# Dilated and sliding attention into a swish layer: the first batch's dilated values used where they land, one load for the tail values, and a new set of scheduling biases

## The chip, the cores and the metric

The kernel runs on one core of a Trainium2 chip. The metric is the device time of one execution in microseconds (us). The core has a matrix engine (TensorE, PE in the profile, with its weight loads as PEld), a vector engine (VectorE, DVE), a scalar engine (ScalarE, ACT), a general engine (GpSimd, POOL) and an engine that here only issues transfers (SyncE, SP). TensorE writes into eight banks of PSUM; the other tiles lie in SBUF. Transfers that change the type from float32 to bfloat16 are issued by POOL, the others by SP.

## What is computed

There are 8 batches of 8 heads, 576 positions and 64 numbers per head. Four heads look at the last 32 positions, four at every fourth one of the last 128. The result is the input of a layer 512 -> 2048 -> 512 with a swish that has its own beta for each of the 2048.

```python
scores = scale * np.matmul(q, k.transpose(0, 1, 3, 2))
rel = pos[:, None] - pos[None, :]
mask_plain = (rel >= 0) & (rel < window)                                   # heads 0 to 3, window = 32
mask_dil = (rel >= 0) & (rel < window * dilation) & (rel % dilation == 0)  # heads 4 to 7, dilation = 4
scores = np.where(masks[None, :, :, :], scores, -1000000000.0)
attn = np.exp(scores - max) / (sum + 1e-09)
x = np.matmul(attn, v)            # then to (4608 tokens, 512)
h = x @ w_in
g = h * (1.0 / (1.0 + np.exp(-beta * h)))
out = g @ w_out
```

## The kernel before

**Two kinds of work share TensorE.** The layer is cut into nine token tiles of 512. For each tile, 16 slots of four matmuls (L901, 512 columns) make h; ScalarE takes a tanh of each slot (L910) and VectorE multiplies (L915) into `g_t`, of which there are two. Then 4 blocks of 16 matmuls (L936) multiply with `w_out_bf`; the first half of w_out serves the first 8 matmuls of a block, the second half the others. A block's result goes through ScalarE or VectorE (L951, L953) to the output.

**Attention, batch by batch.** Heads 0 to 3 (x = 0, 1) are cut into six blocks of 96 queries. Heads 4 to 7 (x = 2, 3) are taken apart by position modulo 4, so that a dilated window becomes a dense one of 32 in 144 positions; the first 128 of them are one matmul (steps S2, S3, V20 to V31), the last 16 are the "tail" (steps T, U). For batches 0 to 2 (`DIRECT = 3`), keys and queries are loaded by POOL, transposed by TensorE (L483 for the dilated heads, L493 for the others, 36 small "quarter" transposes a time) and copied out. Later batches are cast to DRAM and transposed on the way back by SP. Scores are L697 (dilated), L725 and L761 (plain) and L666 (tail); the exponential is L633 on ScalarE. Batch 0 adds its mask by matmuls (L687, L747, L750); later ones multiply by it (L637, on POOL or VectorE). Values are L802 (dilated), L818 (plain) and L787 (tail); L652 and L653 divide by the sum. For batches 0 and 1 TensorE then transposes the result (L840, L855, L870) into `xT`, the input of L901.

**The sum of the weights** comes with the values: each value tile has a 65th column of ones. Values in float32 land as bfloat16; the dilated ones land dense, in `vd16`, and a copy called `spread` moves them to `vd`, where each block of 64 is followed by the ones. `vt_` holds the tail's values, with the ones in place; two loads fill it, one for either half of the remainders modulo 4 (`c`).

**Who decides the order.** Nothing is written out in the final order. `Plan` holds every operation with the engines that it may run on, an estimated duration, its dependences and a due time `vt`; `run` picks one after the other: each engine's candidates by their start, ties within `NEAR` by due time. `NUDGE` adds a bias in ns to the n-th operation's start before this choice. Loads have an estimated rate and latency in the same way, and a new load of POOL waits until the load eight before it has landed. Where the plan leaves TensorE free in the early part, `filler` issues matmuls on zeros: nine groups of twelve small ones (L1057), then single ones of 256 columns (L1059).

**Groups of instructions that the prediction speaks of.** The first loads in POOL's order are batch 0's queries, keys and values, w_in in three parts with one load of batch 1 between, more of batch 1, w_out's first half, more of batch 1, w_out's second half. SP loads batch 0's dilated keys (into `g_t[1]`, free then), which ScalarE and VectorE cast.

Of the kernel before, what the change touches and what calls it, by code (L numbers as in the profile page):

```python
# [10 lines left out]
ACT = mybir.ActivationFunctionType  # L11
# [29 lines left out]
class Plan:  # L41
# [3 lines left out]

    CAPS = {"h": 4, "p": 4, "o": 3, "z": 4, "a": 8, "s": 5, "w": 6}
    SWITCH = 95
    NUDGE = {6: 2500, 32: -2500, 44: 150, 45: -400, 58: -150, 72: 60, 76: -400, 88: -400, 96: 60,
        98: 150, 104: -2500, 105: 900, 107: 900, 161: 150, 167: 900, 172: 60, 173: 400, 199: -900,
        208: 150, 214: -400, 216: 2500, 221: 900, 223: 150, 234: -400, 238: -150, 239: 150,  # L50
        241: 150, 248: -60, 250: -2500, 257: -400, 259: -400, 264: 60, 275: 900, 277: 400,
        278: -2500, 279: 400, 292: -150, 311: 900, 318: -400, 323: 150, 326: -900, 329: 400,
        333: -400, 337: 60, 342: -900, 347: -400, 363: 2500, 364: -900, 365: -150, 367: -2500,
        372: 400, 379: 60, 380: -400, 383: -150, 390: 400, 392: -2500, 394: -400, 408: -150,
        415: -900, 425: -150, 494: -900, 500: -150, 519: 60, 526: 900, 528: -60, 529: 900,
        535: 900, 538: 2500, 553: 900, 589: -60, 597: -2500, 633: 2500, 661: -900, 663: 400,
        669: 2500, 671: 2500, 680: 400, 681: -400, 684: 150, 685: -150, 807: 400, 916: -60,
        943: 150, 948: 150, 1083: 2500}
    LAT = {"PE": 210, "ACT": 45, "DVE": 45, "POOL": 60, "SP": 0}
    NEAR = {"PE": 40, "ACT": 60, "DVE": 60, "POOL": 60, "SP": 0}  # L60

# [137 lines left out]
def kernel(  # L199
# [10 lines left out]
    nc = tc.nc  # L210
    P = 128
    B, H, S, D = q.shape
# [5 lines left out]
    WIN = 32  # L218
    C = 4
    CT = S // C  # L220
    UT = CT - P
    KTL = UT + WIN
# [11 lines left out]
    DIRECT = 3  # L234
# [14 lines left out]
    plan = Plan(range(8))  # L249
# [6 lines left out]
    def copy(e, out, in_):  # L256
# [25 lines left out]
    ptd = const([P, 2, 2, 4, P], BF16, "ptd")  # L282
# [8 lines left out]
    st = [const([P, 2 * RD * D + 2 * RP * D], BF16, f"st{i}") for i in range(2)]  # L291
    std = [s[0:2 * GD, 0:2 * RD * D].rearrange("p (x e) -> p x e", x=2) for s in st]
    stp = [s[:, 2 * RD * D:].rearrange("p (x e) -> p x e", x=2) for s in st]
    vd16 = const([P, 4, C, D], BF16, "vd16")
    vd16_of = [vd16[:]] * DIRECT + [st[b % 2][:, 0:1024].rearrange(
        "p (h T d) -> p h T d", h=4, T=C) for b in range(DIRECT, B)]
# [8 lines left out]
    vd = [const([P, 4, C, DV], BF16, f"vd{i}") for i in range(2)]  # L305
    vt_ = [const([2 * KTL, 2, 4, DV], BF16, f"vt{i}") for i in range(2)]
# [3 lines left out]
    mm = lambda n: n / 2.4 + 2.5  # L310
# [34 lines left out]
    fill3 = plan.op([("DVE", 500)], t_fill3, vt=-7.8)  # L345
# [5 lines left out]
    fill4 = plan.op([("POOL", 800)], t_fill4, vt=-1.2)  # L351
# [58 lines left out]
    def load(queue, args, deps, vt, kb, rate=.4, issue=750, lat=1100, late=0):  # L410
        return plan.op(
            [(queue, issue)],
            lambda e: dma(queue, *args), deps, vt, dma=kb * 1024 / rate / 1000, lat=lat, late=late)

    def direct_qk(b, z, h0, deps, vt):
        rows, n, dst = ((2 * GD, RD, std) if h0 else (P, RP, stp))
        src = bass.AP(tensor=(k, q)[z].tensor, offset=(k, q)[z][b, h0].offset,
                      ap=[[n * D, rows], [2 * S * D, 2], [1, n * D]])
        return load("POOL", (dst[z], src), deps, vt, 576, .41 if b or not (z and h0) else .29, lat=1100 if b else 1450)

    def first_keys():

# [22 lines left out]

    def direct_vd(b, deps, vt, tdeps=()):
        src = v[b, 4:8].rearrange("h (t T) d -> t h (T d)", T=C)[0:P]
        out = [load("POOL", (vd16_of[b].rearrange("p h T d -> p h (T d)"), src), deps, vt, 512, .39, lat=1450 if b < DIRECT else 4000, late=0 if b <= DIRECT else 4000)]
        for c in range(2):
            src = bass.AP(tensor=v.tensor, offset=v[b, 4].offset + ((P - WIN) * C + c) * D,  # L450
                          ap=[[2 * D, 2 * KTL], [S * D, 4], [1, D]])
            out.append(load("POOL", (vt_[b % 2][:, c, :, 0:D], src), list(tdeps), vt + (1.255 if b == 0 else .02 if b < DIRECT else 0) + .001 + .001 * c, 96, .3, lat=1100 if b < DIRECT else 4000, late=0 if b <= DIRECT else 4000))
        return out

    scratch = {}
# [47 lines left out]
    def war(*keys):  # L503
        return [o for key in keys for o in last.get(key, ())]

    def used(key, o):
        last.setdefault(key, []).append(o)

    def wrote(*keys):
        for key in keys:  # L510
            last[key] = []
# [39 lines left out]
    def attention(b, ld, names, vts):  # L551
# [66 lines left out]
        vdeps["P", 0] = [ld["vp"][0], (fill3, fill4)[kv], fill3]  # L618
        def spread(e):
            copy(e, vd[kv][:, :, :, 0:D], vd16_of[b])  # L620
        o = plan.op([("POOL", 1100), ("DVE", 620), ("ACT", 1030)], spread,
                    [ld["vd"][0], (fill3, fill4)[kv]] + war(("vd", kv)), vt, sbuf=True)
        used("vd16" if b < DIRECT else ("st", kv), o)
        wrote(("vd", kv))
        vdeps["D"] = [o]
        vdeps["T"] = ld["vd"][1:] + [(fill3, fill4)[kv]]

        sdone, vdone, xback = {}, {}, []
# [150 lines left out]
        for name in [n for n in names if n[0] in "VU"]:  # L779
            vt = vt_of[name]  # L780
            g = Group("a")
            if name == "U":
                def values(e, g=g):
                    pv = bank(g)[:, 0:4 * (D + 1)].rearrange("p (h e) -> p h e", h=4)
                    for h4 in range(4):
                        for c in range(2):
                            nc.tensor.matmul(pv[:, h4], lhsT=ptt_of(c, h4), rhs=vt_[kv][:, c, h4, 0:D + 1],  # L787
                                             start=(c == 0), stop=(c == 1))
                vop = plan.op([("PE", 8 * mm(D + 1))], values, [sdone["T",]] + vdeps["T"], vt, acquire=g)
                used(("vt", kv), vop)  # L790
                used(("pt", "T"), vop)
                normed("U", vop, g, vt, C * UT, 4,
                       lambda g=g: bank(g)[0:C * UT, 0:4 * (D + 1)].rearrange("p (h e) -> p h e", h=4),
                       xdt[:].rearrange("p x h d -> p (x h) d"), "xdt")
                continue
            x, j = int(name[1]), int(name[2])
            if x >= 2:
                def values(e, x=x, j=j, g=g):
                    pv = bank(g)[:, 0:4 * (D + 1)].rearrange("p (r h e) -> p r h e", r=2, h=2)
                    for r in range(2):  # L800
                        for a in range(2):
                            nc.tensor.matmul(pv[:, r, a], lhsT=ptd[:, x - 2, j, 2 * r + a],  # L802
                                             rhs=vd[kv][:, 2 * (x - 2) + a, 2 * r + j, 0:D + 1],
                                             start=True, stop=True)
                vop = plan.op([("PE", 4 * mm(D + 1))], values, [sdone[x, j]] + vdeps["D"], vt, acquire=g)
                used(("vd", kv), vop)
                used(("pt", x, j), vop)
                normed((x, j), vop, g, vt, P, 4,
                       lambda g=g: bank(g)[:, 0:4 * (D + 1)].rearrange("p (r h e) -> p r h e", r=2, h=2),
                       xdm[:].rearrange("p (r c) x h d -> p c r x h d", c=2)[:, j, :, x - 2], "xdm")  # L810
                continue

            def values(e, x=x, j=j, g=g):
                pv = bank(g)[:, 0:6 * (D + 1)].rearrange("p (m h e) -> p m h e", m=3, h=2)
                for a in range(3):
                    for h2 in range(2):
                        lhs = pt_all[:, at_once(x, 3 * j + a, h2)] if b >= AT_ONCE else pt[x][:, (3 * j + a) * 2 + h2]
                        nc.tensor.matmul(pv[:, a, h2, :], lhsT=lhs,  # L818
                                         rhs=vp[kv][:, (2 * x + h2) * NI + 3 * j + a, 0:D + 1],
                                         start=True, stop=True)  # L820
            parts = sorted({at_once(x, 3 * j + a, h) // 4 for a in range(3) for h in range(2)})
            vop = plan.op([("PE", 6 * mm(D + 1))], values,
                          ([sdone["P", n] for n in parts] if b >= AT_ONCE else [sdone[x, j, 0], sdone[x, j, 1]])
                          + vdeps["P", x], vt, acquire=g)
            used(("vp", kv), vop)
            for key in [("pt", "P", n) for n in parts] if b >= AT_ONCE else [("pt", x, i) for i in range(3 * j, 3 * j + 3)]:
                used(key, vop)
            normed((x, j), vop, g, vt, QT, 6,
                   lambda g=g: bank(g)[0:QT, 0:6 * (D + 1)].rearrange("p (m h e) -> p m h e", m=3, h=2),
                   xsp[j][:, :, x], ("xs", x, j))  # L830
# [262 lines left out]
```

## Time and profile before

| | |
|---|---|
| Time, median of 3 runs | 299.92 us (299.8 to 299.94) |
| The profiled execution's own time | 299.95 us |
| Its span | 298.3 us |
| Clock that TensorE was granted | 0.999 |
| TensorE busy | 293.0 us, 98% |
| VectorE, ScalarE, POOL busy | 186.1, 169.8, 90.4 us |
| First L901 starts | 18.44 us |
| First L936 starts | 34.81 us |
| Last L936 of the long run at the end starts | 294.95 us |

A matmul's duration in the profile includes the time through the array: a matmul of 512 columns is listed with 368 to 376 ns, but four in a row take 0.86 us, 216 ns from start to start. So work is counted by the spacing, and "busy" says only that TensorE always had something under way. Times in an answer count from the start of the span. In the waits, the columns are the total in us, the number of times and the longest; in the chain, start and length in us; in the timeline, start, length, engine, line, operation, tiles and number, and in brackets the idle time before and what ended it.

### The profile page before, as it was taken

To read this page: it belongs to the slowest core of one execution; us is meant where nothing else is said; L and a number is where in the kernel's file an instruction comes from. 1 tells how busy PE (TensorE), PEld (TensorE's weight loads), DVE (VectorE), ACT (ScalarE), POOL (GpSimd) and SP (SyncE) were. 2 spreads that over 40 slices of the span, in tenths; PEclk is the share of its full clock that TensorE was granted. 3 is DMA by queue.
4 is the path that set the end of the run, shared out by engine and by line. 5 is a ranking of instruction groups with operands and counts; after the bars stand their busy time and mean duration, and the time that the engine had idled before them with its cause. 6 is when DMAs were issued, how large, how long until landed. Compare 5 with 4: busy or idle time off the path is not lost.

```text
span 298.3 us, 6224 instructions
## 1 busy us (share of the span) xinstructions
PE 293.0 (98%) x2424; PEld 149.8 (50%) x2424; DVE 186.1 (62%) x422; ACT 169.8 (57%) x308; POOL 90.4 (30%) x126
## 2 busy tenths in 40 slices
PE   8999999999999999999999999999999999999995
PEld 6765456545554445444544454445444444444454
DVE  4879668888767658774589358936891075433300
ACT  3768876867456738642487348634862376445311
POOL 8987354654283026600551065000100000000000
PEclk9999999999999999999999999999999999999999
DMA  7999999999979995999999989995115200010122
GB/s 150 187 208 202 206 196 210 154 163 184 185 124 226 151 199 124 171 136 240 184 188 155 200 174 196 162 186 147 38 31 124 73 0 36 35 37 37 63 76 73
DMA packets 111249, 42.00 MB, mean 141 GB/s; under 512 B 87620, under 2 KB 104596, under 8 KB 111220
## 3 DMA queue, kind: packets, MB, share of 16 engines
q0 software_dynamic: 60336, 18.58, 59.6%
q1 hardware_dynamic: 50740, 22.95, 36.4%
q8 instruction: 19, 0.31, 0.4%
q10 hardware_dynamic: 144, 0.07, 0.1%
q14 instruction: 10, 0.08, 0.1%
HBM read 37.76 MB, written 18.87 MB: 190 GB/s over the span
## 4 chain that ended last, share of the span: by engine, by line
PE 86%; DMA 8%; POOL 2%; DVE 1%; issue 1%; ACT 0%; POOLq 0%
PE bank L936 42%; PE bank L901 36%; DMA w_out_bf<-in_moe_w_out_dram 6%; DMA w_in_bf<-in_moe_w_in_dram 2%; PE bank L818 2%; PE bank L697 1%; PE bank L802 1%; PE bank L725 1%; POOL vp L408 1%; PE bank L787 1%; PE bank L666 0%; PE bank L761 0%; POOL st L408 0%; DVE g L915 0%; PE bank L493 0%
## 5 line engine op out<-in xcount | busy, mean ns | idle before, releaser
L936 PE MATMUL bank<-w_out_bf,g 128*128 128x512 bf16 (+2 forms) x608 | 136.6, 368 | 0.4 <-DMA w_out_bf<-in_moe_w_out_dram 0.4
L901 PE MATMUL bank<-xT,w_in_bf 128*128 128x512 bf16 (+2 forms) x584 | 134.8, 376 | 0.1
L915 DVE SCALAR_TENSOR_TENSOR g<-tnh,bank 128x512 bf16<-128x512 bf16 x144 | 96.5, 683 | 51.5 <-ACT tnh L910 50.3
L910 ACT ACTIVATE tnh<-bank,beta_half 128x512 bf16<-128x512 f32 x144 | 98.4, 690 | 53.2 <-PE bank L901 47.4
L901 PEld LDWEIGHTS <-w_in_bf 128*128 128x128 bf16 x584 | 55.1, 98 | 60.6 <-issue 0.2
L936 PEld LDWEIGHTS <-g 128*128 128x128 bf16 x608 | 55.2, 98 | 57.8 <-DMA w_out_bf<-in_moe_w_out_dram 0.5
L951 ACT ACTIVATE osb<-bank 128x512 f32<-128x512 f32 (+1 forms) x30 | 17.6, 592 | 34.1 <-PE bank L936 29.5
L633 ACT ACTIVATE ptd<-bank 128x512 bf16<-128x512 f32 x32 | 17.0, 600 | 21.4 <-PE bank L697 21.4
L633 ACT ACTIVATE pt<-bank 128x384 bf16<-128x384 f32 (+1 forms) x54 | 21.1, 463 | 6.5 <-PE bank L725 4.1
L637 DVE TENSOR_TENSOR pt<-pt,mask_n 128x384 bf16<-128x384 bf16 (+1 forms) x39 | 14.5, 378 | 12.1 <-ACT pt L633 11.6
L653 DVE TENSOR_TENSOR xsp<-bank,rcp 96x384 bf16<-96x384 f32 x32 | 17.7, 554 | 1.1
L637 DVE TENSOR_TENSOR ptd<-ptd,mask_d 128x512 bf16<-128x512 bf16 x25 | 10.9, 448 | 11.3 <-ACT ptd L633 10.4
L953 DVE TENSOR_SCALAR osb<-bank 128x512 f32<-128x512 f32 (+2 forms) x8 | 4.9, 607 | 20.5 <-PE bank L936 20.5
L652 DVE RECIPROCAL rcp<-bank 128x4 f32<-128x4 f32 (+2 forms) x72 | 12.8, 177 | 3.5 <-PE bank L818 1.4
L408 POOL DMA_DIRECT2D vt<-in_v_dram x16 | 13.7, 864 | 4.0 <-DMA w_out_bf<-in_moe_w_out_dram 2.9
L637 POOL TENSOR_TENSOR pt<-pt,mask_n 128x288 bf16<-128x288 bf16 (+1 forms) x7 | 5.3, 764 | 31.2 <-ACT pt L633 31.2
L653 DVE TENSOR_TENSOR xdm<-bank,rcp 128x256 bf16<-128x256 f32 x32 | 13.6, 424 | 1.1
L408 POOL DMA_DIRECT2D s<-in_k_dram x10 | 12.9, 1286 | 0.6 <-issue 0.6
L1015 POOL COPY pace<-xT 1x2 bf16<-1x2 bf16 x4 | 0.7, 176 | 39.2 <-DMA xT<-x 39.2
L408 POOL DMA_DIRECT2D s<-in_q_dram x10 | 12.2, 1220 | 0.1
L818 PEld LDWEIGHTS <-pt 128*128 128x128 bf16 x192 | 8.9, 97 | 4.4
L408 POOL DMA_DIRECT2D vp<-in_v_dram x9 | 10.2, 1129 | 1.0 <-DVE g L915 0.8
(113 smaller groups left out, 186.8 us busy)
## 6 DMA issues: line engine op xcount, KB each, us to landing
out_dram<-osb SPq DMA_DIRECT2D x35, 256.0 KB, 3.8
s<-in_q_dram POOLq DMA_DIRECT2D x10, 288.0 KB, 10.2
s<-in_k_dram POOLq DMA_DIRECT2D x10, 288.0 KB, 9.0
w_out_bf<-in_moe_w_out_dram POOLq DMA_DIRECT2D x2, 1024.0 KB, 17.4
vp<-in_v_dram POOLq DMA_DIRECT2D x7, 288.0 KB, 13.5
st<-in_q_dram POOLq DMA_DIRECT2D x6, 288.0 KB, 10.0
x<-xsp SPq DMA_DIRECT2D x12, 144.0 KB
st<-in_k_dram POOLq DMA_DIRECT2D x5, 288.0 KB, 13.2
```

Source lines behind the costliest of these rows:

```text
L408: {"POOL": nc.gpsimd, "SP": nc.sync}[queue].dma_start(out=out, in_=in_)
L633: nc.scalar.activation(out=w(), in_=sc(), func=ACT.Exp, scale=SCALE)
L637: E[e].tensor_tensor(out=w(), in0=w(), in1=m(), op=ALU.mult)
L652: nc.vector.reciprocal(out=r, in_=p[..., D])
L653: nc.vector.tensor_tensor(out=dst, in0=p[..., 0:D], in1=r.unsqueeze(len(p.shape) - 1).to_broadcast(list(p.shape[:-1]) + [D]), op=ALU.mult)
L818: nc.tensor.matmul(pv[:, a, h2, :], lhsT=lhs, rhs=vp[kv][:, (2 * x + h2) * NI + 3 * j + a, 0:D + 1], start=True, stop=True)
L901: nc.tensor.matmul(bank(g)[:, a:z], lhsT=w_in_bf[:, kt, fb * P:(fb + 1) * P], rhs=xT[:, kt, xo + a:xo + z], start=(i == 0 and kt == kts[0] ...
L910: nc.scalar.activation(out=th[:, 0:n], in_=bank(g)[:, 0:n], func=ACT.Tanh, scale=beta_half[:, fb:fb + 1])
L915: nc.vector.scalar_tensor_tensor(out=g_t[t % 2][:, fb, c0:c0 + n], in0=th[:, 0:n], scalar=1.0, in1=bank(g)[:, 0:n], op0=ALU.add, op1=ALU.mult)
L936: nc.tensor.matmul(bank(g)[:, lo:hi], lhsT=g_t[t % 2][:, fb, tb * P:(tb + 1) * P], rhs=w_out_bf[:, fb, lo:hi], start=(fb == 0), stop=(fb = ...
L951: nc.scalar.mul(out=ob[:, lo:hi], in_=bank(g)[:, lo:hi], mul=0.5)
L953: nc.vector.tensor_single_scalar(out=ob[:, lo:hi], in_=bank(g)[:, lo:hi], scalar=0.5, op=ALU.mult)
```

## The change

1. For batch 0, `spread` is left out. The dilated values' matmuls read `vd16` directly (64 columns), and the sum of the weights comes from a matmul of its own with the same weights and the column of ones in `vd` (1 column). That is 16 more matmuls, each with its weight load. Other batches do as before. `vd16` is then free only when batch 0's values have been computed.
2. The two loads of tail values of a batch become one, with the same rows of 64 numbers.
3. Estimated rates: batch 2's keys and queries .36 instead of .41, its dilated values .33 instead of .39.
4. A new table of biases, and with it another order of all work.

```diff
-    NUDGE = {6: 2500, 32: -2500, 44: 150, 45: -400, 58: -150, 72: 60, 76: -400, 88: -400, 96: 60,
...
+    NUDGE = {6: -400, 16: -2500, 50: 900, 53: -2500, 54: -400, 58: -2500, 62: -400, 70: 900, 87: -2500,
...
-        return load("POOL", (dst[z], src), deps, vt, 576, .41 if b or not (z and h0) else .29, lat=1100 if b else 1450)
+        return load("POOL", (dst[z], src), deps, vt, 576, .36 if b > 1 else .41 if b or not (z and h0) else .29, lat=1100 if b else 1450)
...
-        out = [load("POOL", (vd16_of[b].rearrange("p h T d -> p h (T d)"), src), deps, vt, 512, .39, ...)]
-        for c in range(2):
-            src = bass.AP(tensor=v.tensor, offset=v[b, 4].offset + ((P - WIN) * C + c) * D,
-                          ap=[[2 * D, 2 * KTL], [S * D, 4], [1, D]])
-            out.append(load("POOL", (vt_[b % 2][:, c, :, 0:D], src), list(tdeps), vt + ... + .001 * c, 96, .3, ...))
+        out = [load("POOL", (vd16_of[b].rearrange("p h T d -> p h (T d)"), src), deps, vt, 512, .33 if b == 2 else .39, ...)]
+        src = bass.AP(tensor=v.tensor, offset=v[b, 4].offset + (P - WIN) * C * D,
+                      ap=[[2 * D, 2 * KTL], [D, 2], [S * D, 4], [1, D]])
+        out.append(load("POOL", (vt_[b % 2][:, :, :, 0:D], src), list(tdeps), vt + ... + .001, 192, .3, ...))
...
-        o = plan.op([("POOL", 1100), ("DVE", 620), ("ACT", 1030)], spread, ...)
-        ...
-        vdeps["D"] = [o]
+        if b:
+            o = plan.op([("POOL", 1100), ("DVE", 620), ("ACT", 1030)], spread, ...)
+            ...
+            vdeps["D"] = [o]
+        else:
+            vdeps["D"] = [ld["vd"][0], fill3]
...
-                            nc.tensor.matmul(pv[:, r, a], lhsT=ptd[:, x - 2, j, 2 * r + a],
-                                             rhs=vd[kv][:, 2 * (x - 2) + a, 2 * r + j, 0:D + 1],
-                                             start=True, stop=True)
+                            lhs, at = ptd[:, x - 2, j, 2 * r + a], (slice(0, P), 2 * (x - 2) + a, 2 * r + j)
+                            if b:
+                                nc.tensor.matmul(pv[:, r, a], lhsT=lhs, rhs=vd[kv][at][:, 0:D + 1], start=True, stop=True)
+                                continue
+                            nc.tensor.matmul(pv[:, r, a, 0:D], lhsT=lhs, rhs=vd16_of[b][at], start=True, stop=True)
+                            nc.tensor.matmul(pv[:, r, a, D:D + 1], lhsT=lhs, rhs=vd[kv][at][:, D:D + 1],
+                                             start=True, stop=True)
```

The order that comes out, at the start. POOL's loads, in their order (b0, b1: the batch; "d" the dilated heads, 96 rows, "p" the plain ones, 128 rows; all keys and queries are 288 KB):

| | before | after |
|---|---|---|
| 1 to 6 | q b0 d, k b0 p, q b0 p, values b0 | the same |
| 7 | w_in first part | the same |
| 8 | q b1 p | q b1 d |
| 9, 10, 11 | w_in second and third part, k b1 d | the same |
| 12 on | vt b0, vt b0, q b1 d, **w_out first half**, k b1 p, values b1 d, **w_out second half** | vt b0, **w_out first half**, k b1 p, q b1 p, values b1 d, **w_out second half** |

The load of q b0 d stands behind the making of `ident_f` before and is POOL's first work of its own after. On TensorE, one set of 36 quarter transposes stands ahead of batch 0's dilated scores after, and behind half of them before; the 36 of q b1 p stand ahead of the first L901 before, and behind w_out's first use after.

## The prediction

> **What bounds the kernel now.** I read the page's engine rows, then TensorE's waits, then the chain that ended last, then the timeline around 18 us.
>
> ```profile
> PE 293.0 (98%) x2424; PEld 149.8 (50%) x2424; DVE 186.1 (62%) x422; ACT 169.8 (57%) x308; POOL 90.4 (30%) x126
> ```
>
> TensorE is busy all the time; the other engines have room on average. So the end moves only with TensorE's own work, its fillers and its stalls. Its waits, over the whole span:
>
> ```profile
> PE bank L936 <- DMA w_out_bf<-in_moe_w_out_dram: 0.4, 1, 0.4
> PE bank L493 <- DMA st<-in_q_dram: 0.2, 1, 0.2
> ```
>
> After the first L901 TensorE stalls in two places. The first is for w_out's first half (start to start, the gap is 0.55 us longer than its neighbours). The second is 0.27 us before 186.28. The chain shows both:
>
> ```profile
> 9.58 6.91 DMA w_in_bf<-in_moe_w_in_dram
> 16.50 0.28 issue
> 16.78 17.99 DMA w_out_bf<-in_moe_w_out_dram
> 34.81 1.04 PE bank L936 x4
> ...
> 183.25 0.70 ACT tnh L910
> 183.97 0.69 DVE g L915
> 184.66 0.96 DVE pt L637
> 185.62 0.61 DVE g L915
> 186.28 2.75 PE bank L901 x12
> ```
>
> The end thus hangs on two numbers: when w_out's first half lands (16.78 + 17.99 = 34.77), and how much matmul work still stands behind that wait. Before it comes the start:
>
> ```profile
> 12.82 0.38 PE L1059 MATMUL bank<-zero 128*128 128x256 bf16 x2
> ...
> 17.22 0.38 PE L1059 MATMUL bank<-zero 128*128 128x256 bf16 x2
> 17.44 0.34 PE L818 MATMUL bank<-vp,pt 128*128 128x65 bf16 x6
> 18.03 0.48 PE L493 MATMUL bank<-ident_b,st 64*64 64x64 bf16 x36 [0.25 <-DMA st<-in_q_dram]
> 18.44 0.82 PE L901 MATMUL bank<-xT,w_in_bf 128*128 128x512 bf16 x3
> ```
>
> L1059 is filler: up to 18 us TensorE has time to give away, afterwards none.
>
> **The named edits.** Dropping batch 0's spread frees VectorE of one copy (0.43 us at 12.03). The 16 extra one-column matmuls load weights again. The nearest rows are L802's: eight take 0.24 us on the chain, 30 ns each, and they load a full tile as these do. So 16 x 30 ns = 0.48 us, and at least 16 x 4 ns = 0.06 us (L697's spacing between matmuls on opposite halves of the array). All of it lies before 18 us, beside fillers of 0.11 us each (nine of them take 1.16 us from 4.09, the last one 0.27), so I cost it at nothing; without that cover it is 0.48 us. [...]
>
> Merging the tail-value loads removes eight issues from POOL's queue (0.71 us median, 5.7 us). POOL is 30% busy and TensorE never waits for it late, so it is worth nothing by itself. It moves the same bytes in the same 128-byte rows: before, the two loads land 0.38 us apart, at 27.18 and 27.56 by the completion records. [...]
>
> **The new biases reorder the start.** The built orders of both kernels, compared engine by engine, show this.
>
> *w_out comes earlier in POOL's queue.* Before, the load is the fifteenth data load of POOL; the three ahead of it are vt, vt and batch 1's dilated queries. After, the queries (96 rows, 288 KB) have taken the place of the 128-row queries ahead of w_in's second part, and the 128-row ones stand behind w_out. So one 288 KB load fewer lies ahead of w_out. The landings of before: vt 27.56, queries 28.94, w_out 34.77. DMA share is 0.93 or more in every half microsecond from 3 to 35 us, so loads land back to back: w_out moves to 34.77 - 1.38 = 33.39. The two query loads that swap took 1.49 (128 rows) and 1.38 (96 rows): 33.28. POOL's first load also stands first now, where it followed a memset and a select (issued at 1.58, POOL's first work at 0.81). That starts the stream up to 0.77 us earlier, at worst not at all. It would share with the SP load of keys, which already fills the engines (0.83 at 2.5 us, 1.07 from 3.0 us), so I take 0.13 us: the room left at 4.0 us (share 0.93) and in the slow ramp. **w_out lands at 33.15, bounds 32.5 and 33.4.**
>
> *TensorE arrives before that.* Between the first L901 and the first L936 the orders hold, at the trace's spacings (216 ns for 512 columns, 30 for 65, 42 for L483, 43 for L870, 27 for L697, 94 for each change between half and full array), 15.76 us before and 14.74 us after. The first L901 after I work out along ScalarE. The first ptd exponential moves from 9.48 to 9.9, since one set of 36 quarter transposes (0.48 us) now precedes the scores. Then come 4 ptd (0.52 to 0.60), qT (0.64), 6 pt (0.36) and 4 xT (0.35 to 0.40): 6.9 us. Waits on TensorE's scores and VectorE's normalising add 0.8. The tail's exponential (0.38), half of qt (0.30) and the batch 1 transposes that waited for their load until 17.99 are out of the way. So 17.6 instead of 18.44; without those waits it would be 16.8, and with nothing gained 18.4. TensorE is ready for w_out at 17.6 + 14.74 + 0.2 (small waits: w_in's last part lands at 25.43, the keys of batch 1 at 26.84) = 32.5, and waits 0.6 us for the load. The gain at the start is thus cut off by the DMA stream.
>
> *More is left behind the wait.* When the first L936 starts, the order after has done 14 of the 16 L901 slots of token tile 0, before all 16. Left over are 8 more L901 (8 x 0.216 = 1.73) and 36 more L493 (0.43), less 8 L697 (0.22) and 2 L840 (0.08): **1.86 us more**. The changes between half and full array are 42 in both.
>
> *Behind it* I compared each load's landing with its first use. w_out's second half is used at 43.3 by this count and lands at about 42.3, as before (the same bytes stand ahead of it). The quarter keys of batch 1 land at 34.4 and are used at 35.0, its quarter queries at 35.9 and 36.6, batch 2's keys at 48.5 and 50.1. All are covered by 0.6 us or more. If a load came later than that, TensorE would lose the excess one for one. One wait is new: POOL's load of batch 2's queries must see w_out's second half landed (42.3), and behind it stands a mask product on POOL (0.76 us) that batch 1's values need at 45.8. With the load's own issue (0.7) it is done by 43.8; from a landing of 44.3 on it would cost.
>
> **Sum.** Before, the profiled run took 299.95, with a span of 298.3 and 1.65 around it; the median of the runs is 299.92. From the first L936 (34.81) to the end of the span are 263.5. After: 33.15 + 0.04 + 263.5 + 1.86 = 298.55, keeping the 0.27 us stall at 186 as the price of one such stall somewhere; + 1.65 = 300.2, against the median 0.03 less. **300.2 us**: 1.62 us earlier at w_out, 1.86 us more behind it.
>
> **Rivals.** *Faster: the start's gain gets through.* If POOL's first load brings the whole stream forward by 0.77, w_out lands at 32.5 and TensorE is just ready: 0.64 less, 299.5; without the stall at 186, 299.2. For it: nothing in POOL's queue stands ahead of that load now. Against it: the DMA engines are full from 3 us on, so the bytes ahead of w_out barely move.
>
> *Slower: the elementwise chain stalls TensorE in each later batch.* The place is the L901 slots behind the burst L725, as at 178.9 to 186.28: ACT has six pt exponentials beside the tanhs, DVE their masks beside the gates, and a bank comes free late. By the same walk I find a margin near zero for the corresponding slot (gate done at 187.0, slot due at 187.0) and 0.3 us in the last batch, where the burst now stands only 2.3 us ahead of its first values (8.3 before). The price is 0.27 each; if four of the later batches pay it more than before, 300.2 + 1.1 = 301.3. It decides from a third such stall on. For it: DVE carries the same 144 gates and 72 normalisings as before, and the order is new. Against it: before, only one of five places stalled.
>
> *The start is late.* If the earlier queries take bandwidth from the SP keys, the casts at 5.46 and all behind them slip. Up to 0.6 us of it hides in the wait for w_out; 1.2 us would give 300.8.
>
> **How the numbers follow.** A measurement of this kernel can tell about 0.2% from no change, 0.6 us. The forecast, within 299.3 to 300.5, gets 0.55. Faster by more needs both the stream moved and the stall gone: 0.15. Slower by more, from stalls or a late start: 0.30. The range goes from 299.3 (w_out at 32.5 and most of the stall gone) to 301.2 (nearly the full price of the stalls, or a late start beside one of them).
>
> **What would show it.** The waits on TensorE should again name w_out, with 0.3 to 0.9 us, with the first L936 at 33.0 to 33.4 and 14 slots done. The first L901 should start between 17.1 and 18.2. Eight issues of vt. The one-column matmuls 20 to 35 ns each. From the first L936 to the end 265.3 us. I am wrong if w_out lands after 34 or before 32.4, if TensorE arrives there without a wait, or if there is more than 0.6 us of stall later.

## The result, and the profile after

| | before | after |
|---|---|---|
| median, us (lowest to highest, runs) | 299.94 (299.64 to 300.65, 18) | 301.62 (299.83 to 303.84, 18) |
| ratio, 95% interval | | 1.0055 [1.0036, 1.0074] |
| profiled run, us (span) | 299.95 (298.3) | 301.52 (299.8) |

The changed kernel is slower by 1.7 us, 0.4 us outside the predicted range, and its runs scatter over 4 us where those of before scatter over 1. The page's engine row is as full as before:

```profile
PE 293.7 (98%) x2440; PEld 150.6 (50%) x2440; DVE 188.1 (63%) x421; ACT 166.7 (56%) x306; POOL 87.0 (29%) x120
```

TensorE's waits (engine, line and releaser, then us in total, times, longest) no longer name w_out. One new wait carries the loss:

```profile
PE bank L911 <- DMA xT<-x: 1.4, 1, 1.4
PE bank L1067 <- DVE warm L316: 1.1, 1, 1.1
PE bank L865 <- DVE xdm L657: 0.3, 1, 0.3
```

The chain of the changed kernel between 95 and 125 us shows where it lies and what leads to it:

```profile
94.68 3.51 SPq L475
...
98.28 3.48 SPq L548
...
101.86 0.54 SPq L966
...
102.49 10.10 DMA xT<-x
...
112.63 1.90 PE bank L911 x8
```

L548 (L547 before) turns batch 3's attention result `x` around into `xT`, in two halves, by transposing transfers that SP issues. L911 needs the second half. It was ready for it at 111.08 (start to start, the gap is 1.545 us too long), and the transfer landed at 112.58. In the kernel before, TensorE came to the same place at the same 111.08 and did not wait: the transfer was issued at 102.25 and had landed at 110.52 by the completion records, 0.56 us ahead. That was the margin. Its chain there:

```profile
110.85 0.22 PE bank L666 x4
111.08 2.59 PE bank L901 x12
```

Two things differ. First, SP's order. The timeline of SP before (start, us, line, operation) has the two halves together and the output store behind them; after, the new biases put the store between them:

```profile
98.70 6.76 SPq L547 DMA_TRANSPOSE xT<-x  x2
105.55 0.54 SPq L956 DMA_DIRECT2D out_dram<-osb  x1
```

```profile
98.28 3.48 SPq L548 DMA_TRANSPOSE xT<-x  x1
101.86 0.54 SPq L966 DMA_DIRECT2D out_dram<-osb  x1
102.49 2.84 SPq L548 DMA_TRANSPOSE xT<-x  x1
```

The store takes 0.63 us of SP's time, about what the margin was. Second, the transfer takes 10.1 us from issue to landing instead of 8.3. So of the 2.1 us by which its landing is later, 0.2 us are a later issue (the transfer ahead of it went out 0.4 us earlier than before, which pays for most of the store) and 1.8 us the longer transfer. The packet records of the trace show what stands beside that: a packet of 16,384 bytes in a queue called "instruction" starts at 109.96 and takes 1.69 us, and at 111.1 twenty 256-byte packets of transposing transfers are in flight at once and take 1.3 us each (no packet of that size moves before the first such transfer, at 59.9 us; the records do not say to which transfer a packet belongs). From 111.5 to 112.25 the DMA share is 0.07, where it is 1.29 in the kernel before. Of the transfer's own 16 completion records one stands at 111.27 and the other 15 at 112.48 to 112.58. Before, the instruction packet came at 112.62, when the transfer was done. The page lists these packets in its third part (queue, then packets, MB, share):

```profile
q8 instruction: 19, 0.31, 0.4%
```

Nineteen packets, beside 4,880 matmuls and weight loads (2440 of each) in the page's engine row. Between the starts of the first packet and the last TensorE began 4,530 of them, 252 a packet on average (164 to 392 from one to the next), and in before 4,514, 251 a packet. If the packets are TensorE's code, that is one for about 250 of its instructions (an estimate; no record names what a packet holds), and 32 more TensorE instructions (the 16 one-column matmuls and their weight loads) would bring each packet earlier.

### The profile page after: what moved, and what is told of

The parts are those of the page before. It is cut to its first block, busy times and chain, and to the rows that moved or that the text cites. A ratio compares the mean times of both kernels' runs of the same rounds, so it can differ in the third digit from the quotient of the medians.

```text
span 299.8 us, 6242 instructions
## 1 busy us (share of the span) xinstructions
PE 293.7 (98%) x2440; PEld 150.6 (50%) x2440; DVE 188.1 (63%) x421; ACT 166.7 (56%) x306; POOL 87.0 (29%) x120
## 4 chain that ended last, share of the span: by engine, by line
PE 91%; DMA 3%; SPq 3%; DVE 1%; issue 0%; DVEq 0%
PE bank L946 40%; PE bank L911 39%; DMA xT<-x 3%; PE bank L828 2%; PE bank L1069 2%; SPq L475 1%; PE bank L701 1%; SPq L548 1%; PE bank L808 1%; PE bank L484 1%; PE bank L1067 1%; PE bank L729 1%; PE bank L494 1%; PE bank L791 1%; PE bank L765 1%; DVE xdm L657 0%
## 5 line engine op out<-in xcount | busy, mean ns | idle before, releaser
L911 PE MATMUL bank<-xT,w_in_bf 128*128 128x512 bf16 (+1 forms) x584 | 135.1, 376 | 1.4 <-DMA xT<-x 1.4
L946 PE MATMUL bank<-w_out_bf,g 128*128 128x512 bf16 (+2 forms) x608 | 135.8, 368 | 0.0
L911 PEld LDWEIGHTS <-w_in_bf 128*128 128x128 bf16 x584 | 54.8, 98 | 61.6 <-DMA xT<-x 1.5
L946 PEld LDWEIGHTS <-g 128*128 128x128 bf16 x608 | 55.5, 98 | 58.6
L961 ACT ACTIVATE osb<-bank 128x512 f32<-128x512 f32 (+1 forms) x32 | 18.9, 595 | 45.4 <-PE bank L946 37.0
L963 DVE TENSOR_SCALAR osb<-bank 128x512 f32<-128x512 f32 (+2 forms) x6 | 3.5, 579 | 19.8 <-PE bank L946 19.8
L408 POOL DMA_DIRECT2D s<-in_q_dram x10 | 14.1, 1413 | 0.0
L408 POOL DMA_DIRECT2D s<-in_k_dram x10 | 11.7, 1165 | 0.5 <-issue 0.3
L408 POOL DMA_DIRECT2D vp<-in_v_dram x9 | 11.6, 1289 | 0.4 <-DMA w_in_bf<-in_moe_w_in_dram 0.3
L828 PE MATMUL bank<-vp,pt 128*128 128x65 bf16 x192 | 10.1, 193 | 0.0
L641 POOL TENSOR_TENSOR pt<-pt,mask_n 128x288 bf16<-128x288 bf16 x9 | 6.5, 747 | 6.5 <-ACT pt L637 6.5
```

Of the source, the lines that this page charges most:

```text
L408: {"POOL": nc.gpsimd, "SP": nc.sync}[queue].dma_start(out=out, in_=in_)
L641: E[e].tensor_tensor(out=w(), in0=w(), in1=m(), op=ALU.mult)
L828: nc.tensor.matmul(pv[:, a, h2, :], lhsT=lhs, rhs=vp[kv][:, (2 * x + h2) * NI + 3 * j + a, 0:D + 1], start=True, stop=True)
L911: nc.tensor.matmul(bank(g)[:, a:z], lhsT=w_in_bf[:, kt, fb * P:(fb + 1) * P], rhs=xT[:, kt, xo + a:xo + z], start=(i == 0 and kt == kts[0] ...
L946: nc.tensor.matmul(bank(g)[:, lo:hi], lhsT=g_t[t % 2][:, fb, tb * P:(tb + 1) * P], rhs=w_out_bf[:, fb, lo:hi], start=(fb == 0), stop=(fb = ...
L961: nc.scalar.mul(out=ob[:, lo:hi], in_=bank(g)[:, lo:hi], mul=0.5)
```

## The experiments

Three theories came out of this. *Packet* (theory 1 and B in the expectations): the added TensorE instructions move the instruction packet into the transfer. *Store* (theory 2): SP's new order delays the transfer. *Spread* (theory A), found in the first profiles below: POOL's spreading copy of batch 3 (`vd<-st`, L257) waits for its load and now stands ahead of the tail queries (`qt<-dq`), which TensorE's tail scores (L670) need. Each run below was timed beside the kernel before on the same chip.

| run | kernel | median, us | ratio to before, 95% |
|---|---|---|---|
| e1 | after, 32 TensorE instructions fewer | 300.59 | 1.0022 [1.0005, 1.0038] |
| e2, e15 | after, store behind | 301.23, 300.16 | 1.0033 [1.0016, 1.0051], 1.0006 [0.9995, 1.0017] |
| e3 | before, 32 more | 300.07 | 0.9996 [0.9986, 1.0005] |
| e4 | before, named edits alone | 299.90 | 0.9992 [0.9980, 1.0003] |
| e5, e14 | after, spread behind | 301.37, 301.41 | 1.0051 [1.0035, 1.0067], 1.0040 [1.0017, 1.0064] |
| e6 | after, spread behind, 32 fewer | 300.75 | 1.0017 [1.0004, 1.0029] |
| e7 | before, 64 more | 301.71 | 1.0053 [1.0033, 1.0073] |
| e8 | before, spread late | 300.39 | 1.0013 [1.0000, 1.0026] |
| e9 | after, spread and store behind | 300.22 | 1.0007 [0.9998, 1.0016] |
| e10 | after, spread and store behind, 32 fewer | 300.23 | 1.0014 [1.0002, 1.0026] |
| e11 | after, batch 0's values as before | 300.88 | 1.0027 [1.0012, 1.0042] |
| e12, e13 | after, again | 302.95, 301.10 | 1.0101 [1.0071, 1.0131], 1.0029 [1.0012, 1.0047] |
| e16 | after, store behind, 32 fewer | 300.58 | 1.0025 [1.0008, 1.0042] |
| e17 | before, store between | 300.43 | 1.0018 [1.0004, 1.0031] |
| e18 | before, store between, 64 more | 302.20 | 1.0071 [1.0048, 1.0094] |

**e4, the named edits alone.** The kernel before, in its own order and with its own biases:

```diff
         def spread(e):
-            copy(e, vd[kv][:, :, :, 0:D], vd16_of[b])
+            if b:
+                copy(e, vd[kv][:, :, :, 0:D], vd16_of[b])
```

Batch 0's matmuls are written as in the changed kernel; of the two tail-value loads the first takes both halves and the second issues nothing.

> The kernel before in its own order and with its own biases, with the two named edits alone: batch 0's dilated values used where they land, with 16 more one-column matmuls (32 more TensorE instructions) and no spreading copy, and one tail-value load in each batch. Theory 1 (instruction fetch): as with 32 more filler instructions, a wait of 0.5 to 1.1 us near 111 and 300.7 (300.3 to 301.1). Theory 2 (the store's place): the biases alone cost the time, so 299.95 (299.6 to 300.2).

299.90 (one of the 12 runs took 1,076 us), no measurable difference. In the old order what the change says it does is free, although it brings the 32 instructions: the packet came at 111.03, and the transfer had landed at 110.08. The loss needs the new order.

**e1 and e3, the packet moved by fillers alone.** This is e1's edit; e3 and e7 use `[32] * 8 + [64] * 8` and `[32] * 16 + [64] * 4`. The columns that the fillers stream stay the same.

```diff
-            for n in range(12):
+            widths = [64] * 12
+            if len(fills) in (2, 3, 4, 5):
+                widths = [128] * 4 + [64] * 4
+            for n, w in enumerate(widths):
```

> The changed kernel with its order and both named edits, but 32 of the 64-column filler matmuls at its start made 16 of 128 columns: TensorE has 32 instructions fewer (its stream is as long as before's), and the same columns. Theory 1 (a fetch of TensorE's instructions falls on batch 3's second transposing transfer and holds it): the tenth 16 KB instruction packet moves from 109.96 to about 112.6 us, that transfer lands near 111 instead of 112.5, the 1.5 us wait of L911 at 112.6 shrinks to under 0.2 us, and the time is 300.0 (299.8 to 300.4). Theory 2 (the output store that now stands between batch 3's two transposing transfers on SP delays the second): nothing changes, the wait stays at 1.2 to 1.6 us and the time at 301.5 (301.2 to 301.9).

> The kernel before, with 16 of the 64-column filler matmuls at its start made 32 of 32 columns: TensorE has 32 instructions more, and the same columns; neither the named edits nor the new biases. Theory 1 (instruction fetch): the tenth packet moves from 112.62 to about 109.5 us, into batch 3's second transposing transfer, which lands at 111.6 to 112.2 instead of 110.45; L901's wait at 111.08 becomes 0.5 to 1.1 us and the time 300.4 to 301.1 (300.7). Theory 2 (the store's place): 299.95, as before (299.7 to 300.2).

In e1 the packet went to 114.09 us and the transfer took 7.5 us, although the store stood between the halves; L911 did not wait, and the median is 300.59. But the profile had a new wait of 1.65 us, at 78 us. Its chain:

```profile
73.48 3.24 issue
...
76.74 1.04 POOL vd L257
...
77.84 0.30 POOL qt L257
...
78.18 0.28 PE bank L670 x4
```

The "issue" of 3.24 us is POOL waiting for batch 3's dilated values, which landed at 76.69. In POOL's queue after, that load stands last, behind the four casts, and its copy ahead of `qt`; before, the load stood second (landed at 61.7) and the copy was long done. In the changed kernel's profile the load landed at 74.75 and L670 came through just in time (1.46 us later, at 76.2; its place is 76.3): a second margin of nothing. In e3 the packet moved forward to 111.31, by 1.3 us and not by the 3 us expected; the transfer had landed at 110.78. So e3 misses, and tells nothing for or against the packet in the transfer.

**e2 and e15, the store behind the second half.**

```diff
-            o.fn(e)
+            if getattr(o, "store", 0) and self.last_xt == (3, 0):
+                self.held_back.append((o, e))
+            else:
+                o.fn(e)
```

What is held back is issued right behind the transfer of batch 3's second half.

> The changed kernel with one SP instruction moved: the output store that stands between batch 3's two transposing transfers is issued behind the second. Theory 1 (instruction fetch): the transfer is issued about 0.6 us earlier (101.9), but the fetch at 109.96 still falls into it; it lands at 111.5 to 112.3, 0.4 to 1.2 us of wait are left, the time is 300.4 to 301.2. Theory 2 (the store's place): it lands at 110.5 as in the kernel before, no wait over 0.1 us, and the time is 300.0 (299.8 to 300.3).

> The changed kernel with the output store behind batch 3's second transposing transfer; the tail queries are still held on POOL, and the instruction packet can still fall into the transfer. 301.2 (300.8 to 301.8).

e2 and e15 are the same kernel on two chips. In e2's profile the transfer was issued 0.9 us earlier than in the changed kernel (101.62) but the packet at 110.37 still fell into it: landed at 112.22, L911 waited 0.76 us (and L670 0.24). In e15's it was issued at 101.37 and landed at 110.28, 0.3 us after a packet at 109.98. Packets were held at 110.4, and now the output store came late: one of its 16 completion records stands at 110.64, the others at 111.91 to 112.01, where nobody waits. TensorE had no wait there, and the median, 300.16, is that of before and not the 301.2 expected, on a chip where the changed kernel (e13) took 301.10 (the two intervals still touch, at 1.0012 to 1.0017). So moving one instruction of SP is enough where the transfer gets out ahead, as in e15; e2, the same kernel on another chip, stayed 0.3% behind.

**e5, e6, e14: the spread behind the tail queries**, without and with 32 instructions fewer.

```diff
+            if tag == ("spread", 3) and e == "POOL":
+                self.kept.append(o)
```

The copy that is kept is issued right behind POOL's `qt<-dq` of batch 3.

> The changed kernel with one POOL instruction moved: batch 3's spreading copy of the dilated values (vd<-st), which waits for a load that landed anywhere from 74.75 to 76.69 us in the three profiles of this order, stands behind batch 3's padded tail queries (qt<-dq) instead of ahead of them. Theory A (that load's scattered landing holds the tail queries, and through them L670 on TensorE near 76.3 us): no wait of L670 over 0.1 us in the profile, the scatter of the runs shrinks from 4 us to under 2, and the median falls by 0.4 to 1.0 us to 300.6 to 301.2; theory B (the instruction fetch at about 110 us on batch 3's second transposing transfer) keeps the wait of L911 near 112.6, 1.0 to 1.6 us. If neither holds: 301.6, scattered as the changed kernel.

> The same move on POOL, and 32 TensorE instructions fewer by merging 64-column fillers into 128-column ones. Theories A and B together: no wait of L670, the tenth 16 KB instruction packet at 112 us or later, batch 3's second transposing transfer 7.5 to 8.3 us from issue to landing (10.1 with the fetch in it), no wait of L911 over 0.3 us, 300.1 (299.7 to 300.5), the runs within 1.2 us of each other. A alone: as the run without the fillers, with 1.0 us or more of wait near 112.6 and 300.6 to 301.2. B alone: 300.6, scattered over 2.5 us, as with fewer fillers alone.

> The changed kernel with POOL's spreading copy of batch 3 behind the tail queries; only the transposing transfer's margin is left. 301.2 (300.8 to 301.6). If the two add up, the changed kernel beside it minus this run is what the held tail queries cost: 0.4 to 1.5 us. If that difference is under 0.2, they cost nothing beside the other wait.

With the spread behind, no profile shows a wait of L670, but the median does not fall: 301.37 and 301.41, against 301.10 of the changed kernel on e14's chip. The scatter did not shrink either (e5: 299.75 to 301.98; e14: 300.03 to 304.44). Expectation A failed for the changed kernel: the held tail queries are a margin of zero, not the loss. (e5's profile caught its fastest run, in which the transfer landed at 110.86 and nothing waited; in e14's, L921, which is L911 here, waited 0.73 us for it.) e6 against e5, on one chip, is read as the packet's share: 1.0017 against 1.0051, 0.6 us of median, and the intervals do not meet; e14's, of e5's kernel on another chip, does meet e6's. e6 did not reach the 300.1 expected. Its profile shows what the store leaves without a packet (the transfer after the store at 102.75, then L921):

```profile
102.75 0.53 SPq L976
...
103.38 8.41 DMA xT<-x
...
111.84 0.39 PE bank L921
```

8.41 us, and a wait of 0.46 us instead of 1.54.

**e9 and e10: both moves**, without and with 32 fewer.

> The changed kernel with two instructions moved: the spreading copy of batch 3 behind the padded tail queries on POOL (theory A), and the output store behind batch 3's second transposing transfer on SP (that transfer is issued 0.6 us earlier); TensorE's instructions as in the changed kernel, so its tenth instruction packet still falls at 108.7 to 110.4 us (theory B). Expected: no wait of L670; L911 near 112 waits 0 to 0.9 us, more where the packet falls later into the transfer; median 300.6 (300.2 to 301.1). If A and the store's place are all there is, 300.0 (299.7 to 300.2).

> The same two moves, and 32 TensorE instructions fewer by merging fillers. All three causes taken away: against the run with the spread behind and 32 fewer (300.75, with 0.46 us of wait at 111.84 and the store between) the second transposing transfer is issued 0.6 us earlier. No wait over 0.15 us of L670 or of L911 near 112, 300.2 (299.8 to 300.5), the runs within 1.2 us. If something else scatters or costs: 300.6 or more.

300.22 and 300.23; e9's runs lie within 0.7 us. With the packet left where it was (109.85), e9 is no slower than before: the transfer, issued at 101.43, landed at 110.12. So the packet is not enough by itself either. It costs where the transfer is late enough to meet what it holds. The waits of TensorE name no transfer and no copy in either but one of 0.5 us in e10, near the start.

**e11: batch 0's values as before**, in the changed kernel's order.

```diff
-                            if b:
+                            if True:
...
+                    if b == 0 and not spreads:
+                        spreads.append(copy("DVE", vd[kv][:, :, :, 0:D], vd16_of[b]))
```

> The changed kernel in its own order, with the first named edit undone: batch 0's dilated values are spread by a copy on VectorE as before, and the 16 one-column matmuls are gone (TensorE has 32 instructions fewer; the merged tail load stays). If the edit matters only by the place of TensorE's instruction packets, this acts as 32 fewer fillers did: 300.6 (300.1 to 301.2), the tenth packet at 112 us or later. If the one-column matmuls cost by themselves, under 300.3 with no wait left. If the edit does not matter at all: 301.6, as the changed kernel.

Batch 0 uses the 65-column matmuls from `vd` again, spread at the first of them. 300.88, the packet at 112.57: as with fewer fillers (e1), and less than the changed kernel on the same chip (e12, 302.95). That fits the reading that the edit matters by its 32 instructions' place in the stream. It does not prove it: the changed kernel on another chip (e13) has nearly the same ratio, 1.0029.

**e12 and e13: the changed kernel again.**

> The changed kernel once more, for its scatter beside these three. Median 301.6 (300.9 to 302.1), runs from under 300.3 to over 302.5. In the profile, the wait of L670 near 76 is the landing of batch 3's dilated values plus 1.46 less 76.3 us (none for a landing before 74.8), and the wait of L911 near 112 is 0.5 to 1.6 us if the instruction packet falls into the second transposing transfer, under 0.4 if not.

> The changed kernel, as the common base of the three runs beside it on one chip. Median 301.6 to 303.0. If the two causes only add up, this is 300.2 plus what each of the two single runs beside it has over 300.2.

Their two profiles are the clearest pair of the study. Same program, nearly the same packet (110.50 and 110.46), but in e12's profiled run SP was 0.8 us earlier. The transfer was issued at 101.75 in e12 and landed at 110.63; in e13 at 102.56, and landed at 112.69. e12's run took 300.04 us, e13's 301.62, and the waits of TensorE are, of e12:

```profile
PE bank L1067 <- DVE warm L316: 1.1, 1, 1.1
PE bank L946 <- issue: 0.5, 3, 0.2
PE bank L911 <- issue: 0.3, 2, 0.2
```

and the first of e13:

```profile
PE bank L911 <- DMA xT<-x: 1.4, 1, 1.4
```

(An "issue" gap of 0.2 us stands where the record of one matmul is missing: in e13's chain seven L911 stand in the 1.91 us from 112.73 on, where eight take 1.90 in after.) The gap before L911 is 1.545 us too long in the first profile, 1.535 in e13's, and none in e12's. Taken off, the three runs are 299.98, 300.09 and 300.04 us. In the profiled executions this one wait is the whole loss, and whether it is paid changes from run to run. The order of the transfers behind this one (`kT` ahead of `qT` after, the other way before) is the same in both executions, so it is not what parts them.

**e16: store behind and 32 fewer**, meant to leave the spread alone.

> The same with 32 TensorE instructions fewer by merging fillers, which moves the instruction packet to about 112.6: only the held tail queries are left. With a scattered landing of batch 3's dilated values (74.7 to 76.7 us) and a wait of landing plus 1.46 less 76.3: 0 to 1.8 us a run, median 300.7 (300.3 to 301.3), scatter over 1.5 us. If it is 300.2 with a scatter under 1.2, the held tail queries cost nothing by themselves.

300.58, scattered from 300.04 to 303.12. The profile has L670 waiting 1.48 us for a load that landed at 76.29, and 0.49 us at 113.09 for the transfer, which SP issued only at 104.36. So the spread can cost. But in the five kernels with 32 instructions fewer in this order, that load landed at 75.0 to 76.7; in the eight profiles with the changed kernel's own instruction count at 74.0 to 75.2, of which L670 waited in one, 0.24 us.

**e7, e8, e17, e18: the causes put into the kernel before.** e7 makes 32 of the fillers 64 of 32 columns; e8 issues batch 3's load of dilated values behind the long casts and the spread ahead of `qt`; e17 issues the store between the halves; e18 is e17 with e7's fillers.

> The kernel before with 64 TensorE instructions more (32 filler matmuls of 64 columns made 64 of 32 columns). With 32 more the tenth instruction packet came at 111.31, just after batch 3's second transposing transfer had landed (110.78). Theory B: it now comes at 109.3 to 110.3, the transfer takes 10 us from issue to landing instead of 7.8 to 8.3, L901 near 111 waits 0.6 to 1.3 us, and the time is 300.6 to 301.2 (300.9). Without B: 300.0 (299.8 to 300.3). If the packet misses the transfer, the run says nothing.

> The kernel before with the changed kernel's place for two POOL instructions: batch 3's load of the dilated values is issued behind the two long casts (it lands near 74 to 77 us instead of 61.7), and the spreading copy that waits for it stands ahead of the padded tail queries. Theory A: L666 near 76.75 waits for POOL in part of the runs (0 to 1.5 us by the landing), the median rises by 0.2 to 0.8 us to 300.2 to 300.8 and the scatter grows from 1.0 to over 1.5 us. Without A: 300.0, scattered by 1 us.

> The kernel before with one SP instruction moved: the output store that followed batch 3's two transposing transfers is issued between them. The second transfer is issued 0.6 us later (near 102.9), the tenth instruction packet stays near 112.6, behind its landing (111.0 to 111.4, 7.6 to 8.9 us after the issue). The margin of 0.56 us is used up: L901 near 111.1 waits 0 to 0.5 us, median 300.3 (300.0 to 300.6). If the store's place alone is the cause: 1.0 us or more of wait, 301.2 or more.

> The same, with 64 TensorE instructions more (32 filler matmuls of 64 columns made 64 of 32 columns), which in the kernel before brought the packet into the transfer and the time to 301.7, of which about 1 us lay at the start and 0.9 in the wait. With the store between as well: the transfer takes 9.4 us or more from issue to landing, L901's wait near 113 is 1.2 to 1.8 us, median 302.1 (301.6 to 302.8). If the packet does not add to the store's place: 301.3 or less.

e7: the packet at 111.29 fell into the transfer, 9.5 us from issue to landing, and L901 waited 0.92 us:

```profile
104.04 9.48 DMA xT<-x
...
113.57 2.76 PE bank L901 x12
```

That shows the packet in the transfer in the old order too, though the kernel also started late there (first L936 at 36.56 instead of 34.81), which in the profile costs more than the wait. e17 came out as expected: issued at 102.66, landed at 111.20 with the packet at 112.27, a wait of 0.53 us, and 300.43. The store's place alone costs about half a microsecond (0.1 to 0.9 by the interval). e18 missed: its time is as expected (302.20), but in its profile the packet, at 111.0, came 3.7 us ahead of the transfer's landing, while the store was still landing (to 112.90), and the transfer took 8.7 us; it was issued only at 106.02, behind the late start and a stall of 1.0 us at 56, and L909 (L901) waited 1.85 us. It does not tell whether the two add. e8: the load landed at 74.72, L666 did not wait in the profile, and the ratio gives 0.4 us (0 to 0.8).

## Why the prediction was wrong

*The named edits: right.* Cost at nothing, and e4 shows nothing. The sixteen extra matmuls were put at 0.48 us behind fillers; in the timeline after they take about 27 ns each:

```profile
12.78 0.20 PE L810 MATMUL bank<-vd,ptd 128*128 128x64 bf16 x1
12.82 0.17 PE L811 MATMUL bank<-vd,ptd 128*128 128x1 bf16 x1
12.85 0.19 PE L810 MATMUL bank<-vd,ptd 128*128 128x64 bf16 x1
```

That is near L802's 30 ns.

*w_out: the landing too late, within its bounds.* 32.58, not 33.15. The term was the load's own time: 5.83 us from the landing ahead of it in before, taken over; 5.09 (27.49 to 32.58) after.

*The first L911: 18.26, not 17.6.* The working goes through in another execution: e5's first L921 (the same line) is at 17.67. What differed, as far as the records show, is TensorE's clock at the start. By the trace's clock record full speed came 3.96 us after the start in before, 4.18 in e5, 6.17 in after; twelve L1069 took 2.45 us from 4.16 in after where nine had taken 1.16 from 4.09. From start to start they stand 0.213 us apart up to 6.05 in after and 0.11 from 6.22, and 0.11 from 4.21 on in before. I had held the clock's moment fixed.

*TensorE's wait at w_out: wrong, at no cost.* Ready at 33.12 (18.26 + 14.74 + 0.12) instead of 32.5, and w_out was there. No wait, which I had named as a sign of being wrong; so had I more than 0.6 us of stall later, and 1.5 us came there. The first L946 still fell into its window of 33.0 to 33.4, since the two errors cancel.

```profile
30.50 2.77 PE L911 MATMUL bank<-xT,w_in_bf 128*128 128x512 bf16 x12
33.12 1.89 PE L946 MATMUL bank<-w_out_bf,g 128*128 128x512 bf16 x8
```

*The work behind it: right.* 1.86 us more was predicted. Without waits, the stretch from the first L936 or L946 to the end is 263.17 in the order before (e3, e4) and 265.1 after (e9, e12, e15): 1.94 more. The stall of 0.27 at 186 is gone (in e3 and e4, in the old order, too), and the rival that the elementwise chain would stall in each later batch happened in no profile. So the execution without the new wait is 300.0, and the forecast of 300.2 would have been off by less than the 0.27 us that it kept as the price of one stall.

*The step that failed* is "Behind it I compared each load's landing with its first use … All are covered." The list went up to batch 2's keys and one wait of POOL, and held only POOL's loads. It left out SP's queue: the transfers that bring `x` back as `xT`, the stores between them, and their margins. There the changed kernel's TensorE waited 1.545 us, for the second half of batch 3's `xT`. The trace of before had the number (110.52 against 111.08), and the built orders of both kernels show the store between the halves. At 0.63 us for a store, that step would have moved a margin of 0.56 to zero and put a wait of 0 to 0.5 us, as in e17, into the sum and its range. That alone would have stayed inside the range. The rest of the measured 1.5 us came with the longer transfer and the instruction packet in it; the packet could not have been read off the diff, but before's packet at 112.62, two microseconds behind the landing, was there to see. The same step missed the spread on POOL, which cost little in the changed kernel's own instruction count (0.24 us in one of eight profiles).

*What stays open.* In the changed kernel's order the profiles contain single waits of 1.65 us at most; its runs of 303 to 304 us, one of them with the spread behind (e14), were not caught. The packet's part rests on its timing in the traces, on e6 and e7, and on the pair e12 and e13. It is not one to one: in the twenty profiles 69 of the 78 holds (twelve or more 256-byte packets of over 0.9 us, starting together) begin within 2 us of an instruction packet, but 37 of the 106 instruction packets that came amid transposing transfers (over 200 of their packets in the next 2 us) were followed by none. What decides that is not known. Nor is it known why the changed kernel's median moved from 301.1 to 302.95 between chips, other than that the wait is a matter of tenths in when SP issues.

## What to carry to other kernels

When an order changes, write down for every transfer that the busy engine waits for, on every queue and up to the end, its landing, its first use and the difference, and compare that list between the two orders; a margin under a microsecond is a price with a chance, not "covered". On a queue that is shared between transfers with a deadline and stores without one, the store goes behind: between them it cost 0.1 to 0.9 us here (e17), with TensorE 98% busy. Where a kernel's runs scatter four times as widely as its predecessor's, as here, look for a wait that hangs on a race of tenths: a single profile shows only one outcome of it.

## What the runs showed of the hardware

- The tenth 16 KB instruction packet was followed, 0.4 to 1.2 us later, by 1.2 to 1.5 us in which some twenty transposing packets of 256 bytes in flight were held (after, e2, e7, e13, e14). Where it came 1.8 to 2.6 us ahead of the landing, batch 3's second transposing transfer took 9.5 to 10.6 us from issue to landing, otherwise 7.5 to 9.3. An exception: e5's packet, at 108.66 and 2.2 us ahead, was followed by held packets too, and the transfer took 8.4.
- The tenth packet moved with the number of TensorE's instructions: in the changed kernel's order it came at 108.7 to 110.5 us, with 32 instructions fewer at 112.6 to 114.3; in the order before it came at 112.3 to 112.8, with 32 or 64 more at 111.0 to 111.3. An edit of 32 instructions in batch 0 (112.57 without it in e11, 109.96 to 110.50 with it in after, e12 and e13) thus moved the packet that meets a transfer of batch 3.
- By the clock record TensorE reached full speed between 3.96 us (before) and 7.85 us (e7) after the start in different executions. The first L911 (L921 in e5) started at 17.67 us in e5, with full speed from 4.18, and at 18.26 in after, with full speed from 6.17.
